# A two-part layer on one core: where the last chunk's left-over products are summed, and the order of the setup

## The chip, the core and the metric

The kernel runs on one core of a Trainium2 chip. The core has a matrix engine (PE, with its weight loads shown apart as PEld), a vector engine (DVE), an activation engine (ACT), GpSimd (POOL) and SyncE (SP). SP, ACT and POOL each have a queue on which they issue transfers (DMAs); an engine works through its own queue in order and is held up by a row whose operands are not ready. Matrix products are written to PSUM, which the kernel divides into eight banks of 512 float32 per partition; everything else on the core lies in SBUF. The metric is the time of one execution on the device, in microseconds, and kernels are compared by the median of several runs.

## The reference

The output has two halves side by side, 2048 x 576 each, in float32.

```python
# half A: a long convolution by a state-space kernel, per channel
K = einsum("dn,dnl,dn->dl", Cc, exp(dt*A*l), dB).real
y = irfft(rfft(u) * rfft(K)) + u * Dskip
# half B: attention, 32 heads of 18, one shared key and value head
q = (x @ wq).reshape(B, S, H, Dh); k = x @ wk; v = x @ wv
p = softmax(einsum("bhqd,bkd->bhqk", q, k) * Dh ** -0.5)
out = einsum("bhqk,bkd->bhqd", p, v).reshape(B, S, H * Dh) @ wo
```

The change touches half B's setup and its last chunk.

## The kernel before

**Attention.** The 2048 queries are taken in four chunks (`NCH`) of 512 (`CT`), the 32 heads in 16 pairs. For a pair and one of 16 key blocks of 128, PE makes the scores `s` (two banks), ACT takes their exponential into a tile `P`, and PE multiplies `P` by the values, `ops` (`product`, line 680). There are three score buffers (`ps_s`, two banks each), one bank for `ops` (`ps_o`), and one bank `f` (`ps_f`) that all side work shares: query projections, bounds, the convolution's transforms, and the output projection.

The operand of a score has 55 rows: the high part of a query or key, twice, its low part, and a row for a bound that is taken off all scores. Keys lie so in `kaug`, queries in one of nine tiles `aug`, one per head pair. Both are put together by small transfers of 18 x 512 values: the high part `kh` and the low part `kl` for the keys (line 273, six transfers for each of four chunks of keys), `qh`, `ql` and the bound's row `sh` for the queries (lines 354, 356, 380, 382).

**Setup.** `setup` projects the keys (`kps`), the first queries (`q0_0`) and the values (`vps`), five steps each over the inner dimension. `km` and `kmx` give the largest key, `aw` and `up` make the bound, `sh` is its row. `vt` and `vp` turn the values. In the first query unit, the four `qh` transfers of pair 1 and the `sh` rows of pairs 0, 1 and 2 are issued on ACT's queue, the rest on POOL's; the keys are placed on SP's queue.

The setup's own tiles (`xr`, `kh`, `kl`, `vt` and others) come from a pool that is closed behind it, and the pool of the `P` tiles is opened after that:

```python
            with tc.tile_pool(name="setup", bufs=1) as tp:
                cv.setup()
                at.setup(tp, cv)
            cv.open(ctx)
            at.open(ctx)
```

So the first exponential writes into memory of setup tiles and waits for everything that reads them, the transfers of line 273 included.

**Order.** PE, ACT and DVE run in the order in which the Python code emits work: a planner (`fill`, with a clock of estimated costs) interleaves scores, products, the convolution and side work. POOL's and SP's transfers stand in program order too.

**The last chunk's end.** The output projection sums over five groups m of 126 rows (the last 72). For the last chunk it is cut: `outproj_part` sums group m for each of eight blocks (four row tiles t, two column halves n) as soon as its heads are done, always into the shared bank `f`, and DVE adds each to `part` in SBUF. Groups 0 and 1 are done in time; of group 2 some blocks are left when the last product is out. `finish` then does group 3 in the freed score buffers (`fin`, `begin`), inverts the last group's denominators (`rc`, line 519), spreads them by a product with `b4` (`bc`, line 520), scales (line 523), adds the last group's product (`end`) and adds all that to `part` (line 514), row tile by row tile, each followed by its output transfer (line 516).

## Time and profile before

| what | us |
|---|---|
| median of three runs | 1249.77 (1247.04, 1249.77, 1253.19) |
| the profiled execution | 1249.9 |
| its span | 1248.1 |
| PE busy in the span | 1158.3 (93%) |
| ACT busy | 1045.6 (84%) |
| DVE busy | 991.0 (79%) |

The span is what the trace covers; 1.8 us of the execution lie around it. In rows of the timeline the first number is the start in microseconds from the span's start, the second the length, then the engine (`SPq` and `ACTq` are queues that issue a transfer), the line, the operation, the tiles written and read, and how many instructions the row merges. In brackets stands the idle time of the engine before the row and what ended it. A matmul shows here as two records, so a group of four is x8.

### The profile page before, as it was taken

The numbers are of one execution on the slowest core, as the hardware profiler recorded it, in microseconds if no ns is written. First come the engines' busy times: TensorE is split into PE (matmuls) and PEld (weight loads), VectorE is DVE, ScalarE is ACT, GpSimd is POOL, SyncE is SP. The second block draws the span as 40 slices with busy tenths as digits, with TensorE's granted clock in tenths as the row PEclk, the third lists the DMA queues.
The fourth block names the chain that finished last, engine by engine and source line by source line (L and its number), as shares of the span: only waits on it lengthen the run. The fifth ranks groups of instructions, "written<-read, shape, count | busy, mean of one in ns | idle before, by whom it ended". The sixth has DMA issues, their size and how long they took to land.

```text
span 1248.1 us, 32953 instructions
## 1 busy us (share of the span) xinstructions
PE 1158.3 (93%) x13762; PEld 477.2 (38%) x13762; DVE 991.0 (79%) x1612; ACT 1045.6 (84%) x1101; POOL 227.5 (18%) x450
## 2 busy tenths in 40 slices
PE   5799999899899999999999899899899899999997
PEld 1234344344334344344333343344344334344332
DVE  4565996996996897995997896897896897896843
ACT  2489989989998989888999889888888888888882
POOL 2260310321210120230422200230151110020000
PEclk9799999999999999999999999899999999999999
DMA  7521112113121012122123112112023112012011
GB/s 216 178 56 46 30 63 82 31 36 89 29 79 46 29 38 70 63 56 85 44 62 90 28 39 65 58 37 71 24 49 122 44 34 80 10 28 101 28 41 40
DMA packets 56922, 75.35 MB, mean 60 GB/s; under 512 B 19536, under 2 KB 30160, under 8 KB 56256
## 3 DMA queue, kind: packets, MB, share of 16 engines
q1 hardware_dynamic: 35784, 58.22, 14.1%
q0 software_dynamic: 20288, 14.39, 5.3%
q8 instruction: 110, 1.80, 0.6%
q10 hardware_dynamic: 696, 0.58, 0.2%
q14 instruction: 44, 0.36, 0.1%
HBM read 35.28 MB, written 22.54 MB: 46 GB/s over the span
## 4 chain that ended last, share of the span: by engine, by line
PE 65%; DVE 14%; ACT 12%; issue 5%; DMA 3%; SPq 1%; ACTq 0%; DVEq 0%
PE ops L680 27%; PE s L392 19%; ACT P L400 10%; PE q L165 5%; PE op L165 4%; PE kg L994 3%; PE iy L165 2%; DVE tab L95 2%; DVE ks L95 2%; DVE acc L95 2%; DMA xr<-xT 2%; PE hu L165 1%; PE hk L165 1%; PE lk L165 1%; DVE pt L95 1%
## 5 line engine op out<-in xcount | busy, mean ns | idle before, releaser
L400 ACT ACTIVATE P<-s 128x1024 f32<-128x1024 f32 x1024 | 967.8, 1031 | 162.6 <-PE s L392 135.3
L680 PE MATMUL ops<-P,v_sb 128*32 128x512 f32 x4096 | 540.9, 602 | 6.2 <-DVE o L99 6.2
L392 PE MATMUL s<-aug,kaug 55*128 55x512 f32 x2048 | 367.6, 443 | 39.6 <-ACT P L400 36.5
L392 PEld LDWEIGHTS s<-aug,kaug 55*128 55x128 f32 x2048 | 171.1, 185 | 353.2 <-ACT P L400 318.3
L356 POOL DMA_DIRECT2D aug<-qh x252 | 126.8, 513 | 601.2 <-DVE qh L99 335.8
L680 PEld LDWEIGHTS ops<-P,v_sb 128*32 128x32 f32 x4096 | 112.1, 110 | 120.1 <-issue 78.7
L165 PE MATMUL q<-x,wq_sb 128*32 128x256 f32 (+2 forms) x1480 | 108.5, 407 | 5.2 <-DVE sck L95 3.7
L165 PE MATMUL op<-wo_sb,oT 126*32 126x288 f32 (+1 forms) x1152 | 84.8, 409 | 6.7 <-DVE part L95 2.3
L382 POOL DMA_DIRECT2D aug<-sh x61 | 34.7, 577 | 271.3 <-DVE sh L103 270.8
L165 PEld LDWEIGHTS q<-x,wq_sb 128*32 128x32 f32 (+1 forms) x1480 | 48.9, 113 | 65.3 <-issue 39.3
L356 POOL DMA_DIRECT2D aug<-ql x128 | 64.1, 509 | 6.2 <-issue 4.9
L95 DVE TENSOR_TENSOR tab<-tab,tt 128x576 f32<-128x576 f32 (+1 forms) x72 | 59.1, 821 | 1.6
L95 DVE TENSOR_TENSOR tab<-tab 128x576 f32<-128x576 f32 (+1 forms) x72 | 58.9, 818 | 1.0
L95 DVE TENSOR_TENSOR tab<-sum,r 128x576 f32<-128x576 f32 (+1 forms) x72 | 58.7, 816 | 0.0
L95 DVE TENSOR_TENSOR tt<-f,sum 128x576 f32<-128x576 f32 (+1 forms) x72 | 58.7, 815 | 0.0
L95 DVE TENSOR_TENSOR tab<-r,dif 128x576 f32<-128x576 f32 (+1 forms) x72 | 58.7, 815 | 0.0
L99 DVE COPY ksb<-kg 128x192 f32<-128x192 f32 x48 | 17.4, 362 | 50.9 <-PE kg L994 50.4
L165 PEld LDWEIGHTS op<-wo_sb,oT 126*32 126x32 f32 (+1 forms) x1152 | 34.5, 110 | 59.9 <-issue 28.4
L95 DVE TENSOR_TENSOR acc<-acc,pt 128x1728 f32<-128x1728 f32 (+2 forms) x36 | 48.5, 1348 | 0.2
L95 DVE TENSOR_TENSOR pt<-us,ks 128x1728 f32<-128x1728 f32 (+2 forms) x36 | 48.6, 1349 | 0.0
L95 DVE TENSOR_TENSOR sck<-lk,sck 128x384 f32<-128x384 f32 x48 | 24.5, 552 | 27.9 <-PE lk L165 27.9
L994 PEld LDWEIGHTS kg<-tab 128*32 128x32 f32 x2304 | 36.7, 110 | 25.8 <-issue 11.7
(118 smaller groups left out, 1002.2 us busy)
## 6 DMA issues: line engine op xcount, KB each, us to landing
aug<-qh POOLq DMA_DIRECT2D x252, 36.0 KB, 1.9
od<-o SPq DMA_DIRECT2D x31, 256.0 KB
aug<-ql POOLq DMA_DIRECT2D x128, 36.0 KB, 1.9
u<-u SPq DMA_DIRECT2D x12, 384.0 KB
kd<-ksb SPq DMA_DIRECT2D x12, 384.0 KB
kt<-kd SPq DMA_DIRECT2D x48, 96.0 KB
outa<-u SPq DMA_DIRECT2D x12, 384.0 KB
oT<-od SPq DMA_DIRECT2D x16, 252.0 KB
```

The costliest lines, as they stand in the source:

```text
L95: return self.v.tensor_tensor(out, *a, **k)
L99: return self.v.tensor_copy(out, *a, **k)
L165: nc.tensor.matmul(ps[j:e], w[:, j:e], x, start=start, stop=stop, tile_position=(0, j))
L356: q.dma_start(t[b:b + 18, :], src[r:r + 18, :])
L382: nc.gpsimd.dma_start(self.aug[(c, h // 2)][54:119:64, :], sh)
L392: nc.tensor.matmul(ps[:, j, :], self.kaug[r, kb * P:(kb + 1) * P], t[r, :], start=True, stop=True)
L400: nc.scalar.activation(pt, ps, AF.Exp, scale=SCALE)
L680: nc.tensor.matmul(o_ps[32 * j:32 * j + 32, :], self.v[:, kb, :], pts[2 * n + j // 2][:, j % 2, :], start=(kb == 0), stop=(kb == 15), tile ...
L994: nc.tensor.matmul(ps[32 * g:32 * g + 32, d, :], t[:, :32], t[:, 32:], start=(j == 0), stop=(j == 1), tile_position=(0, 32 * g))
```

## The change

**At the end.** Blocks that `outproj_part` has not yet summed are kept in a set `late`. The loop before `finish` no longer sums all of them; it stops as soon as group 0 is done and no sum is half-way. `finish` then sums what is left of groups 0 to 3 in `begin`, in the score buffers. The maximum, the copy and the first reciprocal are emitted first; the first product with `b4` stands on PE behind the first five or more sums, and the second reciprocal and its product behind the first sums of the last row tile.

PE at the end of the program, before; `ops` is the last product, `op` are sums in the shared bank, `fin` sums in score buffers, `bc` the spread denominators:

```order
L680 MATMUL ops_7_14012<-P_15_15_14289,v_sb 32x512 x2
L165 MATMUL op_1_1_2_14305<-wo_sb,oT_13239 32x288 x4
L165 MATMUL op_2_0_2_14311<-wo_sb,oT_13239 32x288 x4
L165 MATMUL op_2_1_2_14317<-wo_sb,oT_13239 32x288 x4
L165 MATMUL op_3_0_2_14323<-wo_sb,oT_13239 32x288 x4
L165 MATMUL op_3_1_2_14329<-wo_sb,oT_13239 32x288 x4
L165 MATMUL fin_14339<-wo_sb,oT_13239 32x288 x8
L165 MATMUL fin_14348<-wo_sb,oT_13239 32x288 x8
L165 MATMUL fin_14357<-wo_sb,oT_13239 32x288 x8
L520 MATMUL bc<-rc_last,b_14006 128x256
L165 MATMUL fin_14339<-w_14005,o_last 32x288 x8
L165 MATMUL fin_0_14381<-wo_sb,oT_13239 32x288 x4
```

The same place now:

```order
L692 MATMUL ops_7_14012<-P_15_15_14289,v_sb 32x512 x2
L165 MATMUL fin_14309<-wo_sb,oT_13239 32x288 x8
L165 MATMUL fin_14310<-wo_sb,oT_13239 32x288 x12
L542 MATMUL bc<-rc_last,b_14006 128x256
L165 MATMUL fin_14311<-wo_sb,oT_13239 32x288 x16
L165 MATMUL fin_14309<-w_14005,o_last 32x288 x8
L165 MATMUL fin_0_14363<-wo_sb,oT_13239 32x288 x8
L548 MATMUL bc<-rc_last,b_14006 128x256
```

The five `op` rows are gone and their matmuls stand in the `fin` rows (five sums ahead of `bc`, four behind it, two in the last tiles); on DVE the five additions that emptied the bank are gone.

**In the setup.** The first chunk of keys is placed, then the bound is finished, then the other three chunks are placed. The product `kmx` stands behind two steps of the values instead of three, the last step behind `up`. The transfers of `qh` for pair 1 and the `sh` row of pair 1 go from ACT's queue to SP's, the `sh` row of pair 2 to POOL's, and that of pair 0 stays on ACT's.

SP's queue in the setup, before (two more such groups of `kh` and `kl` follow, then `wq`):

```order
L877 DMA dsk_342<-dsk 128x192
L273 DMA kaug<-kh 18x512 x4
L273 DMA kaug<-kl 18x512 x2
L273 DMA kaug<-kh 18x512 x4
L273 DMA kaug<-kl 18x512 x2
```

And now, with the same two groups and `wq` behind:

```order
L889 DMA dsk_342<-dsk 128x192
L274 DMA kaug<-kh 18x512 x4
L274 DMA kaug<-kl 18x512 x2
L359 DMA aug_112<-qh_0_254 18x512 x4
L385 DMA aug_112<-sh_0_291 2x512
L274 DMA kaug<-kh 18x512 x4
L274 DMA kaug<-kl 18x512 x2
```

Five rows stand between the first chunk of keys and the others. ACT's queue at the same place, before; `P_0_0` is the first exponential:

```order
L330 ACTIVATE qh_0_266<-q_0_184 126x512
L354 DMA aug_112<-qh_0_266 18x512 x4
L380 DMA aug_111<-sh_0_319 2x512
L380 DMA aug_112<-sh_0_319 2x512
L380 DMA aug_113<-sh_0_319 2x512
L400 ACTIVATE P_0_0_366<-s_0_0_357 128x1024
```

And now:

```order
L266 ACTIVATE kh<-kps 128x512
L335 ACTIVATE qh_0_254<-q_0_184 126x512
L385 DMA aug_111<-sh_0_291 2x512
L405 ACTIVATE P_0_0_366<-s_0_0_357 128x1024
L405 ACTIVATE P_1_0_368<-s_1_0_360 128x1024
```

One transfer is left ahead of the exponentials. Between these places at the two ends, the order of PE, ACT, DVE, SP and POOL is the same as before.

The diff:

```diff
--- before.py
+++ after.py
@@ -261,30 +261,35 @@
         for k in range(5):
             project(kps, 0, k)
             matmul4(nc, self.qps, self.wq[0][:, k, :], x0[:, k, :], start=(k == 0), stop=(k == 4))
-        for k in range(3):
+        for k in range(2):
             project(pv, 32, k)
         nc.scalar.activation(kh, kps, AF.Copy)
         V.tensor_reduce(km[:, 4:5], kps, axis=AX.X, op=ALU.max, apply_absolute_value=True)
         V.tensor_scalar(km[:, 0:4], spread[:, 126:130], km[:, 4:5], None, op0=ALU.mult)
         V.tensor_tensor(kl, kps, kh.bitcast(F32), op=ALU.subtract)
-        for c in range(NCH):
+
+        def place(c):
             for r, t in ((0, kh), (36, kh), (18, kl)):
                 for b in (0, 64):
                     nc.sync.dma_start(self.kaug[b + r:b + r + 18, c * CT:(c + 1) * CT].bitcast(F32), t[32 * c:32 * c + 18, :].bitcast(F32))
+        place(0)
+        pk = self.bank(4, "kmx")
+        nc.tensor.matmul(pk[:126, :], spread[:, 0:126], km[:, 0:4], start=True, stop=True)
+        for k in range(2, 4):
+            project(pv, 32, k)
         self.side_work = side = Stream(self.side(), self.k, 99.0)
         while self.first:
             side.advance()
+        V.tensor_reduce(self.kmax[:126, :], pk[:126, :], axis=AX.X, op=ALU.max)
+        while (0, 1) not in self.ready:
+            side.advance()
+        for c in range(1, NCH):
+            place(c)
 
         for m in range(2, 5):
             V.memset(self.wq[m][0:1, 0, 0:1], 0.0)
             self.load_wq(m)
-        pk = self.bank(4, "kmx")
-        nc.tensor.matmul(pk[:126, :], spread[:, 0:126], km[:, 0:4], start=True, stop=True)
-        for k in range(3, 5):
-            project(pv, 32, k)
-        V.tensor_reduce(self.kmax[:126, :], pk[:126, :], axis=AX.X, op=ALU.max)
-        while (0, 1) not in self.ready:
-            side.advance()
+        project(pv, 32, 4)
         V.tensor_copy(vt, pv)
         vp = self.ps_o.tile([P, CT], F32, tag="o", name="vp").rearrange("p (j n) -> p j n", j=4)
         for j in range(4):
@@ -348,9 +353,9 @@
                 for h in hs:
                     r, b = h * DH - m0, 64 * (h % 2) + row
 
-                    q = nc.scalar if (c, m, pr) == (0, 0, 1) and row < 36 else nc.gpsimd
+                    q = nc.sync if (c, m, pr) == (0, 0, 1) and row < 36 else nc.gpsimd
                     t = self.aug[(c, pr)]
-                    if q is nc.scalar:
+                    if q is nc.sync:
                         q.dma_start(t[b:b + 18, :].bitcast(F32), src[r:r + 18, :].bitcast(F32))
                     else:
                         q.dma_start(t[b:b + 18, :], src[r:r + 18, :])
@@ -376,8 +381,8 @@
         V.tensor_scalar(sh, un[0:2, 0:1].broadcast_to([2, CT]), -1.0, None, op0=ALU.mult)
         for h in range(m0 // DH, (m0 + mn) // DH):
             if h % 2 == 1:
-                if (c, m) == (0, 0):
-                    nc.scalar.dma_start(self.aug[(c, h // 2)][54:119:64, :].bitcast(F32), sh.bitcast(F32))
+                if (c, m) == (0, 0) and h < 4:
+                    (nc.scalar, nc.sync)[h // 2].dma_start(self.aug[(c, h // 2)][54:119:64, :].bitcast(F32), sh.bitcast(F32))
                 else:
                     nc.gpsimd.dma_start(self.aug[(c, h // 2)][54:119:64, :], sh)
                 self.ready.add((c, h // 2))
@@ -485,6 +490,7 @@
                     self.o_left -= 1
                     if m < ms[-1]:
                         yield "p", 0.0, True
+                    self.late.discard((t, n, m))
                 K.v = max(K.v, K.t)
                 if ms[0] == 0:
                     V.tensor_copy(part[:, t, cs], ps)
@@ -504,8 +510,11 @@
         ps = {}
 
         def begin(t, nh, tile):
+
             ps[t, nh] = tile[:, :288]
-            matmul4(nc, ps[t, nh], o[:126, 3, t * P:(t + 1) * P], self.wo[:126, 3, cols[nh]], start=True, stop=False)
+            for m in range(4):
+                if (t, nh, m) in self.late:
+                    matmul4(nc, ps[t, nh], o[:126, m, t * P:(t + 1) * P], self.wo[:126, m, cols[nh]], start=(m == min(x[2] for x in self.late if x[:2] == (t, nh))), stop=False)
 
         def end(t, nh):
             matmul4(nc, ps[t, nh], o_sb[:, t * P:(t + 1) * P], w4[:, cols[nh]], start=False, stop=True)
@@ -515,26 +524,28 @@
             if nh == 1:
                 nc.sync.dma_start(self.a["outb"][c * CT + t * P:c * CT + (t + 1) * P, :], part[:, t, :])
 
-        def invert(f):
-            V.reciprocal(rc[:, half[f]], rc[:, half[f]])
-            nc.tensor.matmul(bc[f], b4, rc[:, half[f]], start=True, stop=True)
-
         def scale(f):
             V.tensor_tensor(o_sb[:, half[f]], o_sb[:, half[f]], bc[f], op=ALU.mult)
-        for t in range(3):
-            tile = self.ps_s.tile([P, 2, CT], F32, tag="s", name=f"fin{t}")
-            for nh in range(2):
-                begin(t, nh, tile[:, nh, :])
+        tile = [self.ps_s.tile([P, 2, CT], F32, tag="s", name=f"fin{t}") for t in range(3)]
         for f in range(2):
             V.tensor_scalar(rc[:, half[f]], o_ps[:, half[f]], 1e-37, None, op0=ALU.max)
             nc.scalar.activation(o_sb[:, half[f]], o_ps[:, half[f]], AF.Copy)
             if f == 0:
-                invert(0)
+                V.reciprocal(rc[:, half[f]], rc[:, half[f]])
+
+        sums, n = [(t, nh) for t in range(3) for nh in range(2)], 0
+        while sums:
+            t, nh = sums.pop(0)
+            begin(t, nh, tile[t][:, nh, :])
+            n0, n = n, n + sum(x[:2] == (t, nh) for x in self.late)
+            if n0 < 5 <= n:
+                nc.tensor.matmul(bc[0], b4, rc[:, half[0]], start=True, stop=True)
         scale(0)
         end(0, 0)
         end(0, 1)
         begin(3, 0, self.ps_o.tile([P, CT], F32, tag="o", name="fin3_0"))
-        invert(1)
+        V.reciprocal(rc[:, half[1]], rc[:, half[1]])
+        nc.tensor.matmul(bc[1], b4, rc[:, half[1]], start=True, stop=True)
         end(1, 0)
         end(1, 1)
         add(0, 0)
@@ -590,6 +601,7 @@
             self.busy = True
             if c == NCH - 1 and ms[0] == 0:
                 self.part = self.xp.tile([P, 4, D], F32, tag="x", name="part")
+                self.late = {(t, n, m) for t in range(4) for n in range(2) for m in range(4)}
             if ms[0] == 3:
                 self.w4 = self.p1.tile([P, D], F32, tag="ob", name="w4")
                 self.b4 = self.p2.tile([P, P], F32, tag="aw", name="b4", bufs=1)
@@ -726,12 +738,12 @@
         while behind < len(pairs) // 2:
             product(behind)
             behind += 1
-        while self.todo or self.busy or self.outs or holder():
+
+        while self.todo or self.busy or holder() or any(m == 0 for _, _, m in self.late):
             if self.todo or self.busy:
                 prep.advance()
-            st = holder()
-            if st or self.outs:
-                (st or side).advance()
+            elif holder() or self.outs:
+                (holder() or side).advance()
         conv.drain()
         nc.vector.tensor_scalar(flag, self.ubound[0:1, :], LIMIT / (2 * SCALE), None, op0=ALU.is_le)
         self.finish(NCH - 1, self.part, o_ps, self.w4, self.b4)
```

## The prediction

> **What bounds the kernel now.** I read the totals first, then a table by stage, then the chain of waits and the timeline at the two ends, since the change leaves the order of PE, DVE and ACT alone everywhere between them. The profiled execution took 1249.9 us, 0.13 above the median of the three runs (1249.77; 1247.04 to 1253.19).
>
> ```profile
> span 1248.1 us, 32953 instructions
> PE 1158.3 (93%) x13762; PEld 477.2 (38%) x13762; DVE 991.0 (79%) x1612; ACT 1045.6 (84%) x1101; POOL 227.5 (18%) x450
> ```
>
> ```profile
> 40.50:45.20 4.70, 0.00 (x0) 0.00 (x0) 4.35 (x6) 0.00 (x0) 0.00 (x0) 0.83 0.29 70
> 45.20:53.30 8.10, 6.75 (x40) 2.25 (x40) 0.00 (x0) 5.61 (x6) 0.00 (x0) 0.50 0.92 329
> 60.00:1226.00 1166.00, 1107.06 (x13320) 458.72 (x13324) 951.50 (x1535) 1024.69 (x1079) 214.48 (x423) 0.99 0.18 53
> 1226.00:1243.10 17.10, 13.11 (x176) 5.08 (x167) 10.50 (x20) 0.77 (x2) 0.00 (x0) 1.00 0.11 41
> ```
>
> The columns are the stretch, its length, the busy time of PE, weight loads, DVE, ACT and POOL, the granted clock, the DMA share and GB/s. From 60 to 1226 us PE is busy 1107 of 1166 us; it is the bound, and nothing of that stretch is touched. What can move is the start (PE and ACT do nothing between 40.5 and 45.2 us) and the end (in 1226 to 1243.1 PE stands still for 4 of 17 us).
>
> **The start.** The first exponentials wait for the placement of the keys. The first fence is SP's timeline, the second the chain of waits there, the third three rows of the timeline.
>
> ```profile
> 25.08 3.22 SPq L273 DMA_DIRECT2D kaug<-kh  x4
> ...
> 34.58 2.92 SPq L273 DMA_DIRECT2D kaug<-kh  x4
> ...
> 43.55 1.61 SPq L203 DMA_DIRECT2D wq_sb<-wq  x3
> ```
>
> ```profile
> 42.74 2.08 DMA kaug<-kl
> 44.84 0.04 ACTq L400
> ...
> 45.23 2.86 ACT P L400 x3
> ```
>
> ```profile
> 25.94 4.11 ACTq L354 DMA_DIRECT2D aug<-qh  x4
> 31.46 1.82 ACTq L380 DMA_DIRECT2D aug<-sh  x3
> 45.23 5.61 ACT L400 ACTIVATE P<-s 128x1024 f32<-128x1024 f32 x6 [19.32 <-DVE tab L95]
> ```
>
> SP issues 24 placements back to back; the last starts at 42.74, lands 2.08 us later, and after its waits ACT begins at 45.23. The timeline's own label names DVE, but the chain ends in the placement, and the code agrees: the P tiles lie in memory that the setup's tiles (kh and kl among them) give back, so the first exponential waits until the last placement has read them.
>
> PE meanwhile has done what it can without an exponential:
>
> ```profile
> 36.14 4.32 PE L165 MATMUL q<-x,wq_sb 128*32 128x256 f32 x40
> 46.31 2.62 PE L392 MATMUL s<-aug,kaug 55*128 55x512 f32 x6 [5.86 <-ACT P L400]
> ```
>
> It then waits 5.86 us. All that follows on PE and DVE is queued behind these scores, so a later first exponential moves the whole middle by the same amount.
>
> **The end.** This is the timeline, PE and DVE, of what the change rewrites.
>
> ```profile
> 1224.17 1.90 PE L680 MATMUL ops<-P,v_sb 128*32 128x512 f32 x16
> 1225.88 0.67 PE L165 MATMUL op<-wo_sb,oT 126*32 126x288 f32 x8
> 1227.13 0.69 PE L165 MATMUL op<-wo_sb,oT 126*32 126x288 f32 x8 [0.58 <-DVE part L95]
> ...
> 1230.94 0.69 PE L165 MATMUL op<-wo_sb,oT 126*32 126x288 f32 x8 [0.57 <-DVE part L95]
> 1231.45 3.09 PE L165 MATMUL fin<-wo_sb,oT 126*32 126x288 f32 x48
> 1232.13 0.40 DVE L529 TENSOR_SCALAR rc_last<-ops 128x256 f32<-128x256 f32 x1
> 1232.57 1.75 DVE L519 RECIPROCAL rc_last<-rc_last 128x256 f32<-128x256 f32 x1
> 1234.47 0.70 PE L520 MATMUL bc<-rc_last,b 128*128 128x256 f32 x2
> 1235.21 0.42 DVE L523 TENSOR_TENSOR o_last<-o_last,bc 128x256 f32<-128x256 f32 x1 [0.61 <-PE bc L520]
> 1235.68 1.18 PE L165 MATMUL fin<-w,o_last 128*32 128x288 f32 x16 [0.52 <-DVE o_last L523]
> 1236.68 0.67 PE L165 MATMUL fin<-wo_sb,oT 126*32 126x288 f32 x8
> 1237.35 0.70 PE L520 MATMUL bc<-rc_last,b 128*128 128x256 f32 x2
> 1238.49 0.45 DVE L514 TENSOR_TENSOR part<-part,fin 128x288 f32<-128x288 f32 x1
> 1239.08 0.69 PE L165 MATMUL fin<-wo_sb,oT 126*32 126x288 f32 x8
> 1241.59 1.42 DVE L514 TENSOR_TENSOR part<-part,fin 128x288 f32<-128x288 f32 x3 [0.81 <-PE fin L165]
> ```
>
> A group of four matmuls (eight records) is one sum of one block into one bank. The four sums from 1227.13 to 1230.94 each wait for DVE to empty the single bank: they come 1.27 us apart, while the six fin sums run 0.50 apart (3.02 us from 1231.45 to 1234.47, over six). DVE starts the inversion only at 1232.13, although the last product left PE at 1226.07.
>
> **The change, step by step.**
>
> *Tail.* The five left-over op sums become part of the fin sums, in banks of their own; no product is added or dropped, five DVE additions go. PE: five sums from 1225.88 at 0.50 end at 1228.38. DVE now meets the last product at once: it follows PE by 0.04 (bc ends at 1234.47 + 0.70, the scaling starts at 1235.21), so 1226.11, then 0.44 to the reciprocal (1232.13 to 1232.57) and 1.90 to the bc product (1232.57 to 1234.47): 1228.45, and PE waits 0.07. bc takes 0.70, four more sums 2.0, to 1231.15; the scaling is over long before (0.74 + 0.42 behind bc's start, 1229.61), so the 0.52 wait is gone. The end sums of t = 0 take 1.0 (1235.68 to 1236.68), the two sums of fin3_0 1.0: 1233.15. The second reciprocal follows the scaling and ends at 1231.4 (1229.61 + 1.75), so the second bc waits for nothing; its 0.70 and the end sums of t = 1, 1.0, give 1234.85, just behind the addition that the last tile waits for (scaling 1233.89 to 1234.31, addition to 1234.76). The last tile has two sums instead of one: 1235.85, where the old kernel stood at 1239.08 + 0.50 = 1239.58. Behind it the same work follows. Gain: 3.7. Two hand-overs there have 0.1 us to spare. Ends: only the four bank waits go (4 x 0.57 = 2.3), or all of PE's 4.0 idle goes and with it the trailing 0.2 of lone sums (0.69 against 0.50), 4.5.
>
> The out transfers follow their additions, so the 5 us from 1243.1 to the span's end move whole. The ACT copies of the tail are 0.77 us beside DVE's reciprocals and stay hidden.
>
> *Setup, SP's queue.* Four qh rows and one sh row leave ACT and are issued on SP between the placement of chunk 0 and of chunks 1 to 3; the third sh row goes to POOL. That puts five issues in front of the transfer that releases the first exponential. The price of an issue:
>
> ```profile
> L273 SPq DMA_DIRECT2D kaug<-kh x16: 697/698/932, 25.1 to 41.3; - x16
> L356 POOL DMA_DIRECT2D aug<-qh x12: 498/507/736, 26.2 to 59.8; - x12
> L354 ACTq DMA_DIRECT2D aug<-qh x4: 739/769/1707, 25.9 to 29.3; - x4
> L380 ACTq DMA_DIRECT2D aug<-sh x3: 493/572/617, 31.5 to 32.7; - x3
> ```
>
> In the undisturbed half SP needs 8.97 us for 12 (34.58 to 43.55), 0.748 each; in the first half, beside ACT's issues, 9.50 (25.08 to 34.58), 0.53 more. Between issues stand 0.05 (0.748 less 0.698). Four at 0.748 and one at 0.572 + 0.05 are 3.61; six of ACT's seven issues are gone, so the 0.53 goes too: +3.1. SP has not issued aug before. At POOL's 0.507 (and 0.05) the term is 2.3; at ACT's 4.11 for four, with the first half as slow as now, it is 4.8. The placement has the same queue and the same 18x512 shape, so I stay by it. The first exponential starts at 48.3.
>
> [...]
>
> *Setup, bound and values.* The bound's product comes one value sum earlier on PE and the last value sum goes behind it; the memsets go behind sh. In the rows
>
> ```profile
> 27.77 0.38 PE L282 MATMUL kmx<-km,spread_sb 128*126 128x4 f32 x2
> 28.09 0.62 PE L259 MATMUL vps<-x,wkv_sb 128*32 128x512 f32 x1
> 29.83 0.23 PE L165 MATMUL up<-sel_sb,aw 126*32 126x8 f32 x8
> 30.37 0.41 DVE L103 TENSOR_SCALAR sh<-un 2x512 fp32r<-2x512 f32 x1
> ```
>
> two value sums take 1.74 us (28.09 to 29.83), so sh comes about 0.87 earlier, at 29.9. Worth nothing: the scores it releases then stand still until 48.3. SP reaches its sh row around 32.5, when sh is ready, so it does not stall there; wq, dft, u and wo are issued 3.1 later, but so is their use. POOL's extra row costs it 0.5 us while nobody waits for it.
>
> *Sum.* +3.1 - 3.7 = -0.6: 1249.3 against the profiled 1249.9, 1249.2 against the median.
>
> **Rivals.** A difference of 0.5% (6.2 us here) is about what a measurement of this kernel can tell from no change.
>
> A, the forecast, 1249.2: chance 0.6.
>
> B, the start costs nothing, because the five issues hide or because something else releases the exponential: 1249.8 - 3.7 = 1246.1. For it: the label that names DVE's tables, which SP does not touch. Against it: the chain. 0.12. [...]
>
> C, slower: SP's queue runs slower with the new rows in it. It decides at a last placement after 42.74 + 3.7 = 46.4, that is at a mean step of 0.763 over the 28 steps from 25.08; the step of the first half today is 0.79 (9.50 over 12), so the sign is close. At that step everywhere the last starts at 47.2, +4.5 - 3.7 = +0.8, 1250.6; at the slowest issue seen (0.932 + 0.05) it starts at 52.6, +9.9 - 3.7 = +6.2, 1256.0. 0.17; with the repeats' spread on it, 0.06 of that beyond 0.5%.
>
> D, the first exponential no longer waits for the placement and follows its scores at about 36, when PE turns to the queries: 9 us at the start and 3.7 at the end, 1237. The P tiles still take the setup's memory, so 0.04.
>
> The remaining 0.07 is for what no row shows, both ways.
>
> **How the numbers follow.** Faster beyond 0.5%: D and 0.02 of the rest, 0.06. Slower beyond: 0.06 of C and 0.03 of the rest, 0.09. Within: 0.85. The range: the ends of the terms give -2.2 (2.3 - 4.5) to +2.5 (4.8 - 2.3), so 1247.6 to 1252.3; B reaches down to 1246.1, C up; the repeats of the kernel before lie 2.7 below and 3.4 above its median, so I take 1245.0 to 1254.0, which leaves out D and the upper part of C.
>
> **What would show it.** Right: SP's last placement starts near 45.8, the first exponential near 48.3, PE's wait at its second scores grows from 5.86 to above 8 us; from the last product of ops to DVE's last addition 13.2 us instead of 16.9 (1226.07 to 1243.01); no PE wait for part before the bc product. Wrong: an exponential that starts at 45 or earlier, a PE wait of more than 0.5 us at the first bc product, or a last placement later than 46.4. The sum would also fail if the stretch from the first exponential to the last product changed its length by more than a microsecond or two.

## The result and the profile after

| | kernel before | changed kernel |
|---|---|---|
| median, 22 runs each on the same chip | 1250.07 (1246.27 to 1258.74) | 1252.12 (1247.63 to 1257.13) |
| the profiled execution | 1249.9 | 1251.7 |
| its span | 1248.1 | 1250.0 |
| first exponential starts | 45.23 | 48.31 |
| from there to the end of the last product | 1180.84 | 1183.28 |
| from there to the end of DVE's last addition | 16.94 | 13.16 |
| from there to the end of the span | 5.09 | 5.24 |

The ratio of after to before is 1.0013, 95% interval 0.9999 to 1.0027, that is +1.6 us (-0.1 to +3.4). In the two profiles the stages add up to the same: +3.08 + 2.44 - 3.78 + 0.15 = +1.9. The end gave what was forecast, the start took what was forecast, and 2.4 us more came in the long middle, whose work is in the same order in both.

From the page of the changed kernel, and from its table by stage (same columns as in the prediction, the stretches moved with the work):

```profile
span 1250.0 us, 32945 instructions
PE 1157.3 (93%) x13762; PEld 476.8 (38%) x13762; DVE 989.0 (79%) x1607; ACT 1045.5 (84%) x1101; POOL 227.8 (18%) x451
```

```profile
43.60:48.30 4.70, 0.00 (x0) 0.00 (x0) 0.25 (x1) 0.00 (x0) 0.00 (x0) 0.52 0.31 72
48.30:56.40 8.10, 6.76 (x48) 2.73 (x52) 0.00 (x0) 6.15 (x7) 0.00 (x0) 0.64 0.96 324
63.10:1231.60 1168.50, 1108.68 (x13314) 458.66 (x13310) 950.18 (x1534) 1023.21 (x1077) 212.99 (x420) 0.99 0.18 53
1231.60:1244.80 13.20, 12.07 (x172) 5.52 (x164) 8.42 (x14) 0.77 (x2) 0.00 (x0) 1.00 0.14 51
```

PE's 4 us of idle in the last stage have shrunk to 1.1 of 13.2, and five DVE instructions are gone (1607 against 1612). In front of the first exponential PE, ACT and POOL stand still as before, 3 us later; DVE, which was busy there for 4.35 us before, is through with its work too (0.25).

**The start.** SP's timeline, and below it the chain of waits and three rows of the timeline:

```profile
24.55 3.21 SPq L274 DMA_DIRECT2D kaug<-kh  x4
...
29.42 2.94 SPq L359 DMA_DIRECT2D aug<-qh  x4
32.47 0.56 SPq L385 DMA_DIRECT2D aug<-sh  x1
33.08 3.00 SPq L274 DMA_DIRECT2D kaug<-kh  x4
...
45.03 1.44 SPq L274 DMA_DIRECT2D kaug<-kl  x2
```

```profile
45.77 2.05 DMA kaug<-kl
48.31 2.86 ACT P L405 x3
```

```profile
28.96 0.46 DVE L103 TENSOR_SCALAR sh<-un 2x512 fp32r<-2x512 f32 x1
48.31 5.61 ACT L405 ACTIVATE P<-s 128x1024 f32<-128x1024 f32 x6 [22.93 <-DMA kaug<-kl]
49.39 2.63 PE L397 MATMUL s<-aug,kaug 55*128 55x512 f32 x6 [8.91 <-ACT P L405]
```

The five rows stand where the order had them, 29.42 to 33.08, and cost 3.66 us there. The last placement starts at 45.77 instead of 42.74. The label on ACT's wait, which named a table of DVE in the kernel before, now names the placement: 22.93 us of it. `sh` is ready at 29.42 (28.96 + 0.46), 3 us before SP reaches its row, and nobody gains by that. PE's wait at the second scores has grown from 5.86 to 8.91 us.

**The end**, PE and DVE:

```profile
1231.41 2.61 PE L165 MATMUL fin<-wo_sb,oT 126*32 126x288 f32 x40
1231.66 0.42 DVE L531 TENSOR_SCALAR rc_last<-ops 128x256 f32<-128x256 f32 x1 [1.21 <-PE ops L692]
1232.12 1.75 DVE L534 RECIPROCAL rc_last<-rc_last 128x256 f32<-128x256 f32 x1
1233.98 0.68 PE L542 MATMUL bc<-rc_last,b 128*128 128x256 f32 x2
1234.58 2.15 PE L165 MATMUL fin<-wo_sb,oT 126*32 126x288 f32 x32
1236.55 1.16 PE L165 MATMUL fin<-w,o_last 128*32 128x288 f32 x16
1238.61 0.70 PE L548 MATMUL bc<-rc_last,b 128*128 128x256 f32 x2
1243.34 1.42 DVE L523 TENSOR_TENSOR part<-part,fin 128x288 f32<-128x288 f32 x3 [0.81 <-PE fin L165]
```

Five sums run in one row (x40 is five groups of eight records, 2.61 us). DVE meets the last product at 1231.66, just behind its end (1231.60), and starts the inversion at 1232.12. Between the first `bc` and the end sums there is no wait. From the last product to the last addition (1244.76) it takes 13.16 us.

### The profile page after: what moved, and what is told of

Its sections match the earlier page's. It is cut to its first block, busy times and chain, and to the rows that moved or that the text cites. A ratio compares the mean times of both kernels' runs of the same rounds, so it can differ in the third digit from the quotient of the medians.

```text
span 1250.0 us, 32945 instructions
## 1 busy us (share of the span) xinstructions
PE 1157.3 (93%) x13762; PEld 476.8 (38%) x13762; DVE 989.0 (79%) x1607; ACT 1045.5 (84%) x1101; POOL 227.8 (18%) x451
## 4 chain that ended last, share of the span: by engine, by line
PE 65%; DVE 15%; ACT 11%; issue 5%; DMA 2%; SPq 1%; ACTq 0%; DVEq 0%
PE ops L692 27%; PE s L397 19%; ACT P L405 10%; PE q L165 4%; PE op L165 4%; PE kg L1006 3%; PE iy L165 2%; DVE tab L95 2%; DVE ks L95 2%; DVE acc L95 2%; DMA xr<-xT 2%; PE hu L165 1%; PE hk L165 1%; PE lk L165 1%; DVE pt L95 1%
## 5 line engine op out<-in xcount | busy, mean ns | idle before, releaser
L165 PEld LDWEIGHTS q<-x,wq_sb 128*32 128x32 f32 (+1 forms) x1480 | 48.4, 111 | 63.2 <-issue 37.5
```

The lines of the kernel that those rows point to most:

```text
L165: nc.tensor.matmul(ps[j:e], w[:, j:e], x, start=start, stop=stop, tile_position=(0, j))
```

## The experiments

Times given with a ratio are medians of the runs of five rounds, beside the kernel before on the same chip. Three chips were used, so two experiments are compared by their ratios. In microseconds a ratio is worth 12.5 per 0.01.

**1. The new end alone** (the hunks of `outproj_part`, `finish` and the main loop; the setup as before).

```diff
 in setup, queries:      as in the kernel before
 in outproj_part, finish, the loop behind the last product:  as in the changed kernel
```

> The new end with the old setup. Forecast's theory (the rows ahead of the last key placement delay the first exponential by their issue time, the end gains 3.8 us): first exponential at about 45.2 us, last product to last addition 13.2 us, 3.8 us less than the kernel before at the same granted clock, ratio 0.9970. Rival (the setup costs nothing and the missing gain was lost in the middle): as the changed kernel, ratio 1.001.

Measured: 1248.13, ratio 0.9965 (0.9950 to 0.9981). From the last product to the last addition 13.16 us, to the hundredth what the changed kernel shows. The first exponential, from ACT's timeline of this kernel:

```profile
44.54 5.61 ACT L400 ACTIVATE P<-s 128x1024 f32<-128x1024 f32 x6 [19.14 <-DVE tab L95]
```

So the end is worth 4.4 us (2.4 to 6.3) by the runs and 3.8 by the trace, and the loss of the whole change comes from the setup.

**2. The new setup alone**

```diff
 in setup, queries:      as in the changed kernel
 in outproj_part, finish, the loop behind the last product:  as in the kernel before
```

> The new setup with the old end. Forecast's theory: last placement 21.2 us after the first one's issue instead of 17.7, first exponential 3.1 to 3.6 us later, last product to last addition 16.9 us as before, ratio 1.0025 to 1.0029. Rival (the start costs nothing): ratio 1.000. Rival (the new setup disturbs the stretch between): more than 5 us, ratio above 1.004.

Measured: 1257.85, ratio 1.0043 (1.0027 to 1.0059), +5.4 us. ACT's first row, and one row of PE in the end:

```profile
48.66 5.60 ACT L405 ACTIVATE P<-s 128x1024 f32<-128x1024 f32 x6 [22.93 <-DMA kaug<-kl]
...
1240.44 5.10 PE L165 MATMUL fin<-wo_sb,oT 126*32 126x288 f32 x48
```

The first exponential is 3.4 us late, as expected (48.66 against 45.23). The runs lose some 2 us more than that: the ratio is the one named for the second rival, though its interval just takes in the 1.0027 to 1.0029 of the theory. The trace does not show the loss as a wait. The profiled execution itself is no guide to it: its end took 19.90 us instead of 16.94, because six sums that took 3.09 us in the kernel before took 5.10 here, at a granted clock of 0.60 instead of 1.00. The last section comes back to that.

**3. The kernel before, once more**, as a measure of what a profile says.

```diff
 nothing is changed
```

> The kernel before once more, for the stretch between the first exponential and the last product, which took 1180.8 us in its profile and 1183.3 in the changed kernel's, at granted clocks of 0.985 and 0.983. If only the granted clock moves it: a time that falls by about 1.1 us for every 0.001 of clock, on the line of the changed kernel's runs shifted by less than 2 us, and a middle stretch that differs between profiles of the same kernel by 1 to 4 us. If the change moved it: about 1181 again at whatever clock.

Measured: 1251.17, ratio 0.9991 (0.9973 to 1.0009). The middle took 1181.55 us here against 1180.84 in the first profile of the same kernel, a smaller difference than the 1 to 4 us expected.

**4. The placements no longer hold the exponentials back**

```diff
-        kh = tp.tile([P, CT], F32R, name="kh")
-        kl = tp.tile([P, CT], F32R, name="kl")
+        kh = self.p1.tile([P, CT], F32R, tag="db", name="kh", bufs=2)
+        kl = self.p1.tile([P, CT], F32R, tag="db", name="kl", bufs=2)
```

The pool `p1` stays open, so no `P` tile lies on `kh` or `kl`, and every engine's rows stand in the same order as in the changed kernel.

> The changed kernel with kh and kl in two buffers that are first used again much later, so that the exponentials' buffers no longer lie on them; every row of every engine stands where it stood. Forecast's theory (the last placement releases the first exponential): it starts behind its scores at about 33 us, the second scores at about 40.5 instead of 49.4 (behind the queries' matmuls), 8.9 us less than the changed kernel, ratio to the kernel before about 0.994. Rival (DVE's tables release it, as the timeline of the kernel before says): first exponential at about 44, 4.4 us less than the changed kernel. Rival (something else of the setup holds it): no change.

Measured: 1247.56, ratio 0.9955 (0.9937 to 0.9973). ACT's timeline (first two rows and one later), one row each of PE and DVE:

```profile
32.54 1.02 ACT L405 ACTIVATE P<-s 128x1024 f32<-128x1024 f32 x1 [7.27 <-PE s L397]
...
41.05 2.86 ACT L405 ACTIVATE P<-s 128x1024 f32<-128x1024 f32 x3 [3.64 <-PE s L397]
...
75.08 5.61 ACT L405 ACTIVATE P<-s 128x1024 f32<-128x1024 f32 x6 [8.03 <-PE s L397]
```

```profile
68.88 0.69 DVE L99 CAST qh<-q 126x512 fp32r<-126x512 f32 x1 [11.88 <-DMA aug<-sh]
...
71.04 1.51 PE L1006 MATMUL kg<-tab 128*32 128x64 f32 x48 [5.51 <-DVE ab L107]
```

The first exponential comes 16 us earlier, which settles what held it: the memory of `kh` and `kl` under the `P` tiles. But the ratio is only 0.0058 below that of the changed kernel, some 7 us. Comparing the k-th exponential of both profiles, x4_keep is 11.5 us ahead at the 7th to the 27th, and 4.1 us ahead from the 28th on (75.08 us). A new wait took 7.5 us back. Its chain of waits, and SP's timeline at that place:

```profile
49.48 6.45 DMA aug<-qh
...
56.81 7.93 DMA aug<-qh
...
65.52 3.23 DMA aug<-qh
```

```profile
48.15 0.57 SPq L1158 DMA_DIRECT2D dft_sb<-dft  x1
48.81 0.86 SPq L888 DMA_DIRECT2D u<-u  x2
...
50.27 5.74 SPq L302 DMA_DIRECT2D wo_sb<-wo  x5
```

POOL's transfers for the second query unit now start at 49.5 us instead of 61.0, and run into the 4 MB that SP loads once the placements are out (`wq`, `dft`, `u`, `wo`). A transfer of 36 KB that lands 2.0 us after its issue in the changed kernel (the median there) takes 3 to 8 us in the rows of the chain. Until the last has read `qh`, DVE does not write the next one (11.88 us of waiting), and PE waits behind DVE (5.51 us).

**5 to 7. Moving the large loads out of the way.** Three steps, each with `kh` and `kl` kept; PE, ACT and POOL do the same rows in the same order in all of them, DVE too but for the one-element writes that hold the loads back.

```diff
 x5_wo     load_wo() after query unit 1 instead of at the start of main
 x6_loads  conv.start() (dft, u) and load_wo() after query unit 1
 x9_late   conv.start() after the cast of qh for unit 2, load_wo() after unit 2
+            if wait == 2 and r >= 24:
+                wait = 1
+                conv.start()
+            if wait == 1 and (0, 9) in self.ready:
+                wait = 0
+                self.load_wo()
```

> The changed kernel with kh and kl kept (as in x4_keep), and the 1.3 MB of wo issued after query unit 1 instead of at the start of the main part; every other row of every engine in the same order. x4_keep won 11.5 us up to exponential 15 and lost 7.5 us of it at exponential 27. Theory (the loads of wq, dft, u and wo, 46.5 to 56 us on SP's queue, slow GpSimd's transfers of unit 1, which hold the buffer qh and so the DVE and PE): with 1.3 of 4 MB gone the loads end near 54 us, the cast of qh for unit 2 comes near 65 instead of 68.9 us, the loss at exponential 27 is 3 to 5 us, and the ratio to the kernel before is 0.992 to 0.9935. Rival (GpSimd's 28 issues of about 0.5 us are themselves what is late, whatever is loaded beside them): cast at 68 to 69 us and 0.9955 as in x4_keep.

Measured: 1249.02, ratio 0.9978 (0.9966 to 0.9991); cast of `qh` at 68.97 us, 8.1 us lost at the 28th exponential. Missed: DVE had the row that releases `wo` early in its order, and SP issued it at 53.66 instead of 50.27, still beside the last of POOL's transfers.

> As x5_wo, with dft and u also issued after query unit 1. Theory: only the 0.8 MB of wq (46.5 to about 50 us) is left beside GpSimd's rows, the cast of qh for unit 2 comes at 63 to 64 us, the loss at exponential 27 is at most 1.5 us, first use of dft (95 us before) is not late, and the ratio is 0.989 to 0.991. Rival (GpSimd's issues): 0.9955 as in x4_keep.

Measured: 1247.28, ratio 0.9956 (0.9940 to 0.9973); the cast at 66.60, 6.1 us lost. Missed as well, and for the same reason. In DVE's and SP's timelines of x6_loads:

```profile
66.60 0.69 DVE L99 CAST qh<-q 126x512 fp32r<-126x512 f32 x1 [9.88 <-DMA aug<-ql]
```

```profile
53.81 0.33 SPq L1161 DMA_DIRECT2D dft_sb<-dft  x1
54.24 1.51 SPq L891 DMA_DIRECT2D u<-u  x2
55.85 2.38 SPq L302 DMA_DIRECT2D wo_sb<-wo  x5
```

The loads had moved by 6 us only and fell on the second half of POOL's rows (to 65 us). This did not yet tell the loads from POOL's own pace.

> As x6_loads, with dft and u issued after the cast of qh for unit 2 and wo after that unit. In x6_loads the loads had only moved from 47..56 to 54..60 us, and GpSimd's last rows of unit 1 (56 to 65 us) still landed late: the cast came at 66.6 us, and 6.1 us of the 11.9 won were lost at exponential 27. Theory (large loads beside these rows): now only wq's 0.8 MB is left, the cast comes at 62.5 to 64 us, the loss at exponential 27 is at most 1.5 us, dft is in place before its first use, and the time is 3.5 to 5 us below that of x6_loads: ratio 0.991 to 0.993. Rival (GpSimd's rows are late without the loads too): cast at 66 us or later, ratio as x6_loads, 0.9955.

Measured: 1240.72, ratio 0.9916 (0.9893 to 0.9940). SP's, DVE's and ACT's timelines of x9_late:

```profile
66.17 0.33 SPq L1163 DMA_DIRECT2D dft_sb<-dft  x1
66.60 1.30 SPq L893 DMA_DIRECT2D u<-u  x2
```

```profile
62.34 0.69 DVE L99 CAST qh<-q 126x512 fp32r<-126x512 f32 x1 [5.76 <-DMA aug<-sh]
```

```profile
67.08 5.61 ACT L405 ACTIVATE P<-s 128x1024 f32<-128x1024 f32 x6 [0.54 <-PE s L397]
```

The cast comes at 62.34, ACT's wait at the 28th exponential is 0.54 instead of 8.03 us, and the lead over the changed kernel stays at 12.0 us through it. `dft` is first used at 86.9 us, 20.7 us after SP issued it (66.17). This shows that the loads, beside POOL's transfers, were the new wait.

**8 and 9. The same with the old setup.** x8_best is x6_loads with the setup of the kernel before, x10_late_old is x9_late with it.

```diff
 in setup, queries:      as in the kernel before, with kh and kl from p1
 the end, and the times of the loads: as in x6_loads, x9_late
```

> The new end with the old setup, kh and kl kept, and the loads of dft, u and wo after query unit 1: as x6_loads, but with the setup of the kernel before. If the reordered setup is worth anything once no exponential waits for the last placement, this is slower than x6_loads; by the rows, ACT issues five transfers (3.6 us) ahead of its first exponential here, which then starts near 33.5 instead of 32.5 us, but the second pair's rows land at the same 34 to 35 us: I expect the same as x6_loads within 0.0015 in the ratio, 0.989 to 0.991. Rival: the old setup holds the first exponentials by 2 us or more, ratio 0.9915 or above.

Measured: 1242.46, ratio 0.9933 (0.9918 to 0.9949). The expected 0.989 to 0.991 was missed, as that of x6_loads, because the loads still met POOL's rows. It lies 0.0023 below x6_loads, with intervals that overlap.

> As x9_late, with the setup of the kernel before. By the theory the same step at exponential 27, at most 1.5 us, and 3.5 to 5 us below x8_best: ratio 0.9885 to 0.9905; within 0.0015 of x9_late if the order of the setup is worth nothing here. Rival as in x9_late: 0.993.

Measured: 1236.97, ratio 0.9889 (0.9867 to 0.9911), the fastest version of all, 13.9 us below the kernel before by the ratio. From ACT's timeline:

```profile
35.00 2.85 ACT L400 ACTIVATE P<-s 128x1024 f32<-128x1024 f32 x3 [9.34 <-PE s L392]
...
67.24 5.61 ACT L400 ACTIVATE P<-s 128x1024 f32<-128x1024 f32 x6 [0.54 <-PE s L392]
```

ACT has seven issues in front of its first exponential here (four `qh` and three `sh` rows, as in the kernel before; the expectation of x8_best counted five), and from the 4th to the 49th exponential the two setups are level within 0.2 us. So the order of the setup gains nothing with the memory wait gone either; the difference of 0.0027 to x9_late lies within the intervals.

**10. The changed kernel with the five rows back on ACT's queue** and the rest of the change as it is, but for the `sh` row of pair 2, which goes back from POOL's queue to ACT's as well.

```diff
-                    q = nc.sync if (c, m, pr) == (0, 0, 1) and row < 36 else nc.gpsimd
+                    q = nc.scalar if (c, m, pr) == (0, 0, 1) and row < 36 else nc.gpsimd
...
-                if (c, m) == (0, 0) and h < 4:
-                    (nc.scalar, nc.sync)[h // 2].dma_start(
+                if (c, m) == (0, 0):
+                    nc.scalar.dma_start(
```

> The changed kernel with the five rows of the first query unit (4 aug rows and one sh row) back on ACT's queue, and everything else of the change kept: the new order of the setup and the new end. If the five rows on SP's queue are what moves the first exponential (my forecast's step), the last placement is at 42.0 to 42.8 us, the first exponential at 44.5 to 45.3, the second scores at 45.5 to 46.4, and the ratio is that of x1_tail, 0.995 to 0.998. Rival (the new order of the bound, the values' sums and the placements costs the time itself): first exponential at 47 to 48.5 us and a ratio of 1.000 to 1.002.

Measured: 1246.92, ratio 0.9961 (0.9947 to 0.9975). ACT's and PE's timelines:

```profile
45.20 5.61 ACT L405 ACTIVATE P<-s 128x1024 f32<-128x1024 f32 x6 [19.49 <-DMA kaug<-kl]
```

```profile
46.28 2.62 PE L397 MATMUL s<-aug,kaug 55*128 55x512 f32 x6 [7.60 <-ACT P L405]
```

The first exponential is back at 45.20 and the ratio is that of the new end alone. The whole cost of the setup is the five rows on SP's queue; the new order of bound, values' sums and placements costs and gains nothing that shows.

**11 and 12. The delay by itself.** The kernel of experiment 1 with five, and with ten, more transfers ahead of the placements, whose data nobody reads.

```diff
+        for j in range(5):
+            nc.sync.dma_start(spare[j // 5][18 * (j % 5):18 * (j % 5) + 18, :].bitcast(F32),
+                              kh[32 * (j % 4):32 * (j % 4) + 18, :].bitcast(F32))
```

> The kernel x1_tail (old setup, new end) with five further transfers of 18x512 on SP's queue ahead of the placements, whose data nobody reads: the changed kernel's delay of the first exponential alone, without its order. The traces put the start of the changed kernel 3.8 us later than x1_tail, but the ratios differ by 6 us (1.0013 against 0.9965), and x2_setup stands to the kernel before likewise (3.4 and 5.4 us). Plain theory: the first exponential moves by 3.5 us and the time by 3.5 us, ratio 0.9993. Rival (a longer standstill of the matmul engine at the start costs as much again later, through the granted clock): time by 5.5 to 6.5 us, ratio 1.001 to 1.002, granted clock 0.982.

> As x11_five with ten such transfers. Plain theory: first exponential 7.1 us later than in x1_tail, ratio 1.0022. Rival (the granted clock adds to it in proportion): 11 to 12 us, ratio 1.005 to 1.006. If the clock adds a fixed amount once the standstill is long enough: ratio 1.0035 to 1.004.

Measured: five, 1253.21, ratio 1.0010 (0.9995 to 1.0025); ten, 1257.19, ratio 1.0051 (1.0031 to 1.0072). SP's and ACT's first rows, with five and then with ten:

```profile
24.66 3.97 SPq L272 DMA_DIRECT2D spare<-kh  x5
...
48.17 5.61 ACT L403 ACTIVATE P<-s 128x1024 f32<-128x1024 f32 x6 [22.68 <-DMA kaug<-kl]
```

```profile
24.69 7.67 SPq L272 DMA_DIRECT2D spare<-kh  x10
...
52.09 5.61 ACT L403 ACTIVATE P<-s 128x1024 f32<-128x1024 f32 x6 [26.57 <-DMA kaug<-kl]
```

| kernel (all with the new end) | first exponential, us | ratio to before |
|---|---|---|
| x1_tail | 44.54 | 0.9965 |
| x7_queue | 45.20 | 0.9961 |
| x11_five | 48.17 | 1.0010 |
| changed kernel | 48.31 | 1.0013 |
| x12_ten | 52.09 | 1.0051 |

The plain values, 0.9993 and 1.0022, lie outside both intervals, the first only just; they start from x1_tail's ratio, which has an interval of its own (0.9950 to 0.9981). A weighted line through the five points has a slope of 1.6 us of time per us of delay (1.2 to 2.0, from the intervals of the five ratios). So in the runs a delay here costs more than itself, and it does so without any of the changed order.

Where the rest lies in the profiles, the trace's record of the granted clock tells. In the profiles of the kernel before and of the changed kernel it holds 1.00 and 0.50 and nothing between them, the 0.50 (half rate) for 25.6 and 29.6 us of the stretch in the table. This is the stretch from the first exponential to the end of the last product, in the eight kernels whose first exponential waits for the placements:

| kernel | first exponential, us | the stretch | of it at half rate | the stretch less half of that |
|---|---|---|---|---|
| x1_tail | 44.54 | 1182.41 | 25.4 | 1169.7 |
| x3_before | 45.18 | 1181.55 | 26.6 | 1168.3 |
| x7_queue | 45.20 | 1180.93 | 23.9 | 1169.0 |
| kernel before | 45.23 | 1180.84 | 25.6 | 1168.0 |
| x11_five | 48.17 | 1186.39 | 36.3 | 1168.3 |
| changed kernel | 48.31 | 1183.28 | 29.6 | 1168.5 |
| x2_setup | 48.66 | 1185.45 | 31.9 | 1169.5 |
| x12_ten | 52.09 | 1182.30 | 25.3 | 1169.6 |

A straight line through the eight has 0.46 us of length per us at half rate. Less half of that time, the stretch is the same within 1.7 us and does not grow with the start. So no wait beyond that size is added in it by a later start; what differs between these profiles beyond the delay is, within 1.7 us, time at half rate. Whether a later start brings more of such time is not shown: the three kernels that start near 48.4 have more of it, x12_ten, which starts last, has not (its profile is that of its fastest run).

The runs have a clock too, as a mean: 0.9842 and 0.9862 in x1_tail and x7_queue, 0.9820 and 0.9824 in x11_five and the changed kernel, 0.9815 in x12_ten. From the mean of the first two (0.9852) to that of the next two (0.9822) that is 0.0030 of about 1250 us, 3.75 us of clock. A standstill 3.4 us longer at half clock (the rows above have 0.52) makes 1.7 of that, in time in which nothing is computed; 2 us are left, of an excess of 2.7. For ten transfers the same reckoning leaves 0.0037 x 1250 - 3.6 = 1 us where 4 are missing, with an interval of 2.6 us either way on that ratio alone. So the clock fits the excess of five rows and not clearly that of ten. As the cause of the excess in the runs it is not shown. In the other direction no such factor was seen: x10_late_old is 9.4 us ahead of x1_tail from the 13th exponential on and 0.0076, 9.5 us, in time, with an interval of some 3 us either way.

## Why the prediction was right

*The forecast.* 1249.2 in a range of 1245 to 1254 with 0.85 on no change, against 1252.12 and a ratio whose interval takes in 1. On the difference: -0.6 forecast, +1.6 measured (-0.1 to +3.4), so the forecast difference itself lies just outside the interval; the range and the choice of no change held, the size of the difference did not.

*The end.* The step held line by line. Five sums at 0.50 took 2.61, the reciprocal came 0.52 behind the last product's end, the wait of 0.52 before the end sums is gone, and the whole took 13.16 where 13.2 was worked out. Experiment 1 shows the gain without the rest. Both hand-overs with 0.1 us to spare came out on the right side.

*The start.* The chain was read rightly: the last placement releases the first exponential, through the memory of `kh` and `kl` (experiment 4), and the five rows in front of it are the whole price (experiment 10). The last placement at 45.8 (45.77), the first exponential at 48.3 (48.31) and PE's wait above 8 us (8.91) are as forecast. One term failed: the 0.53 us that SP's first half was to gain once ACT's issues had left. The rows from the first placement to the last took 17.66 us before (25.08 to 42.74) and 21.22 after (24.55 to 45.77), +3.56, which is the 3.61 without any relief; and the first four placements take 3.21 us with ACT silent, as they took 3.22 with it busy. So the slow first rows were not ACT's doing. That the point in time agreed is luck: the placements began 0.53 us earlier in this profile; with the changed kernel's setup they begin at 24.43 to 24.90 in the kernels here, with the old one at 24.56 to 25.08.

*The middle.* "Nothing of that stretch is touched", and so its change was set to nothing. That is the step that failed: it was 2.4 us longer in the profile, more than the microsecond or two that the forecast named as its limit. The order of the work is the same, as was said, and no new wait shows. What moved is the granted clock, which the sum has no term for: 29.6 us of the stretch ran at half rate against 25.6 before, and half of that difference is 2.0 of the 2.4 (table in experiments 11 and 12). In the runs a later start costs about 1.6 times its delay by experiments 11 and 12; the 5.4 us of experiment 2 for a delay of 3.4 agree, but their interval (3.4 to 7.4) takes in the delay alone. Whether the later start itself brings the time at half rate stays open. The two parts run apart add up to the whole: -4.4 (experiment 1) + 5.4 (experiment 2) = +1.0, against +1.6 measured. The start was forecast at +3.1 and is worth 5.4 in the runs; the traces show 3.1 to 3.4 of it as a wait.

*The rivals.* B, a start that costs nothing, falls with experiment 10: taking the five issues off SP's queue brings back 3.1 us. An issue of a placement takes 0.70 us of SP in both profiles, 29 rows stand one behind the other now, and only the last one's 2.05 us of transfer adds to them. C decided at a last placement after 46.4; it came at 45.77, and the 17 steps from 33.08 to there take 0.746 us each, as in the undisturbed half before, so C's mechanism, a slower queue, did not come. The small loss that came, which was C's outcome, came in the middle. D, an exponential that waits for its scores alone, is not what the change does; experiment 4 made it so, and found that D's price was too high by itself: of 11.5 us at the start, 7.5 went at once to a wait that the placement had hidden. Only with the large loads moved was D's 9 us and more to be had (x10_late_old).

## What to carry to other kernels

When a wait at the start is removed, look at which transfers the late start had kept apart: here 4 MB of loads and 25 small transfers that hold a buffer met only after the fix, and the gain came when the loads were put behind the point where that buffer was free. A transfer's place in SP's queue had a price of its own here, 0.75 us, because the chain of waits ended in a later entry of that queue, and memory given back by a closed pool was what ended it, though no line of code names the wait (with `kh` and `kl` kept, the first exponential started at 32.54 instead of 48.31 us). Where a stretch whose work is unchanged differs by a few microseconds between two profiles, compare its time at half rate before looking for a wait. Parts of opposite sign are best run apart: the new end alone was 0.35% faster, and the whole change not at all.

## What the runs showed of the hardware

**Half-rate stretches in a busy kernel.** The same 16 matmul records, at the same place of the order, in the timeline of the kernel before and in its table by stage:

```profile
324.49 1.92 PE L680 MATMUL ops<-P,v_sb 128*32 128x512 f32 x16
```

```profile
320.10:323.50 3.40, 2.68 (x32) 0.93 (x24) 3.37 (x2) 3.39 (x4) 0.00 (x0) 1.00 0.00 0
324.40:326.40 2.00, 2.00 (x20) 0.48 (x18) 1.98 (x3) 2.00 (x3) 0.00 (x0) 1.00 0.00 0
```

and in the same two views of the changed kernel:

```profile
327.10 3.60 PE L692 MATMUL ops<-P,v_sb 128*32 128x512 f32 x16
```

```profile
323.70:327.10 3.40, 2.24 (x14) 0.56 (x6) 3.33 (x4) 3.39 (x5) 0.00 (x0) 1.00 0.00 0
327.00:330.70 3.70, 3.70 (x20) 0.66 (x18) 3.67 (x5) 2.48 (x3) 0.00 (x0) 0.54 0.00 0
```

In the changed kernel's profile the granted clock is 0.54 for 3.7 us while PE is busy all of that time, and the 16 records take 3.60 us instead of 1.92. Just ahead of it, from 323.70 to 327.10, PE was busy for 2.24 of 3.40 us: it waited for ACT between single scores (0.42 us ahead of those at 325.77 and 326.68). In the kernel before, PE was busy for 2.68 of 3.40 us from 320.10 and for 2.99 of 3.40 from 323.50, and the granted clock stayed at 1.00.

Up to the last addition the two profiles hold 14 half-rate stretches, six in the kernel before and eight in the changed one. In the 3.41 us ahead of each, PE was busy for 2.25 us or less. It was as little busy elsewhere without half rate behind it: for 1.72 of the 3.41 us from 688.68 in the kernel before, with the granted clock at 1.00 there and in the 3.41 us that follow. What decides which of these places half rate follows is not shown here; that these stretches are why two profiles of one kernel differ is an inference.

The exponentials of the two profiles keep a constant distance for long and jump at some eight places, by 0.6 to 1.7 us mostly, once by 2.65, and in either direction. Two profiles of the kernel before differ too, by 0.7 us in the length of the stretch (1180.84 and 1181.55) and by 1.0 us in its time at half rate (25.6 and 26.6). In 22 runs of the changed kernel the times go from 1247.6 us at a mean clock of 0.987 to 1257.1 at 0.978, about 1 us per 0.001, so a stage of 1180 us cannot be compared to a microsecond between two single profiles.

**Small transfers beside large ones.** Transfers of 36 KB issued by POOL, which landed in 2.0 us in the changed kernel, took 3 to 8 us in the chain of experiment 4, while SP's loads of 4 MB came in (256 GB/s between 49.5 and 66.0 us).
